# Four products at two levels instead of three, in three of the four down stages of a two-layer kernel

## The chip, the cores and the metric

The kernel runs on one core of one Trainium2 chip. Its time is the device time of one execution in microseconds, as the median of several runs. A profile is one more execution, recorded by the hardware profiler. The engines are TensorE (PE, matmuls; PEld are its weight loads), VectorE (DVE), ScalarE (ACT), GpSimd (POOL) and SyncE (SP), which issues every DMA of this kernel in one queue, in program order.

## The reference, cut to what matters

A layer of linear attention (A) and a gated layer (B) stand in turn, twice, each behind a layer norm and with a residual. The change touches layer B only. Here x is 2048 x 1024, w_gate and w_up are 1024 x 3584, w_down is 3584 x 1024, all in bf16.

```python
def _B_ref(x, w_gate, w_up, w_down):
    g = jnp.einsum("bsd,df->bsf", x, w_gate)
    u = jnp.einsum("bsd,df->bsf", x, w_up)
    h = g * u
    return jnp.einsum("bsf,fd->bsd", h, w_down)

x = A_x
x = x + _A_ref(_layernorm(x, axis=-1), A_wqkv, A_wo)
x = x + _B_ref(_layernorm(x, axis=-1), B_w_gate, B_w_up, B_w_down)
x = x + _A_ref(_layernorm(x, axis=-1), A_wqkv, A_wo)
x = x + _B_ref(_layernorm(x, axis=-1), B_w_gate, B_w_up, B_w_down)
```

## The kernel before

**How it is put together.** Every instruction is added by `_Prog.add` (line 50) to the queue of its engine, in the order of the program text; `plan` (line 105) then works out from the ranges that each one reads and writes which semaphores it has to wait for. Nothing is reordered. So the order of the `P.add` calls is the order on each engine, and a DMA whose wait is long holds up all DMAs that were added after it.

**The stages.** Layer B works on the tokens in two halves of 1024. For each half a gate/up stage (`gateup`, line 1786) makes h in the tile blocks hA, hB, hC, hD (two halves of tokens by two halves of the 3584 columns), and a down stage (`down`, line 1864) multiplies h by w_down and adds the result to x. The text calls the four down stages D0 (first layer B, first half), D1 (first layer, second half), D2 and D3 (second layer). Behind D0 and D2 comes the gate/up stage of the second half, behind D1 the second layer A; D3 ends the kernel.

**Seven products.** Each 2 x 2 block product is done with seven block products in place of eight (Strassen-Winograd). They are numbered 1 to 7; a down stage takes them in the order of the string in `DPROD` (line 730). At one level a product is 4 tiles of 128 tokens by 14 matmuls of 512 columns (line 2154), accumulated in one PSUM bank a tile; the banks run on from product to product in a chain, and after some products a bank's sum leaves PSUM: `stt` (line 841) on DVE scales it, adds a tile of x (or an earlier sum) and writes an f32 tile `rtmp` or x itself. For the products that `DTWO` (line 731) names, each of the blocks is split once more in seven (`two_level`, line 2016): 98 matmuls of 256 columns (line 2049). That needs sums of the blocks of h (`a_sums`, line 1902, four DVE operations a product, into the buffers of `s_buf`, line 1894) and sums of the blocks of the weights. Chosen so before: no product of D0, and products 5, 3 and 2 of D1, D2 and D3.

**The weights.** The four blocks of w_down and the four one-level sums of them (products 5, 6, 7 and 4) are in DRAM; the latter, the scratch tensor `t_scratch`, are made during the first gate/up stage (`wd_load`, `wd_prep`, `wd_store`, lines 939 to 952). `ring_issue` (line 785) loads the next weight unit into one of five slots of 8 KB a partition: half a one-level product (896 KB, written 4/0 and 4/1 below), or one of four parts a to d of a two-level one (3136 KB together). The sums for the second level lie in a further scratch tensor, `d_scratch`, one block a product, and are made once: those for 5 and 3 during D0 (`b_load`, `b_sums`, `b_store`, lines 1921 to 1952, called from `prep_step`, line 1977), those for 2 in D1 from weights loaded for that purpose (`b2_prep`, line 1954). An entry "-" in the list of units (`d_units`, line 736) takes a slot and loads nothing.

**What else runs in these stages.** Tiles of x are stored to a scratch tensor (`stash`, line 751) and loaded again in the `tail` of the next gate/up stage (line 1846), since the room is wanted for other things meanwhile. `sp_load` (line 775) fetches the sums of x for the next gate/up stage's second level. In D2 `x_pop` (line 871) runs the operations of `x_ops` (line 860), which make the sums of the normalized x for the next gate/up stage; `t1` to `t4` are the four of 2048 elements a partition. `dticks0` (line 2228) is called after each tile of D0 and D2 and `dticks1` (line 2257) after each tile of D1 and D3; they hold these loads, stores and pops. `tt` (line 838) is a DVE operation of two tensors, `dma` (line 439) the helper under which all DMAs appear.

## Time and the profile before

| | |
|---|---|
| time, median of 3 runs | 1435.49 us (1435.11 to 1437.32) |
| span of the profiled execution | 1433.4 us |
| that execution's clock of TensorE | 1.000 over the whole span |
| busy PE / DVE / ACT / POOL | 1422.9 / 1140.8 / 700.2 / 225.6 us |
| mean DMA rate, share of 16 engines | 230 GB/s, 76.8% |
| D0, D1, D2, D3 start at | 402.24, about 652, 1109.57, 1350.01 us |

The span is the profiled execution's own time from its first to its last instruction; the page gives no other time for it. It lies 2.1 us under the median of the runs. A busy time is a sum over the stages; whether an engine has room in one stage is read from that stage's window. In section 5 of the page a group is a line of the code, an engine and an operation, with busy time, mean of one in ns and the idle time before it with what ended it. L839 is the line of `tt`, L842 that of `stt`, L440 that of `dma`, so these groups hold operations from many places, and are told apart by their tiles and forms.

### The profile page before, as it was taken

The page shows a single profiled execution, that of the slowest core. Times are in us where ns is not written, and L with a number is a line of the kernel's source. Part 1 is how long each engine was busy: PE and PEld are TensorE (multiplying, and loading weights), DVE is VectorE, ACT ScalarE, POOL GpSimd, SP SyncE. Part 2 cuts the span into 40 slices and gives each one's busy share as a digit, 9 for nine tenths or more (in the row PEclk, how much of TensorE's full clock was granted, in tenths as well). Part 3 has the DMA queues.
Part 4 walks back from the last instruction along what each step waited for, and adds up shares of the span by engine and source line. Part 5 has one row for each costly group of instructions (what it writes and reads, how often), then busy time and mean ns, then how long its engine had stood idle before and what let it go on. Part 6 is the DMA issues. An engine that isn't in the chain of part 4 may idle for free.

```text
span 1433.4 us, 22057 instructions
## 1 busy us (share of the span) xinstructions
PE 1422.9 (99%) x8248; PEld 801.1 (56%) x8304; DVE 1140.8 (80%) x2048; ACT 700.2 (49%) x1478; POOL 225.6 (16%) x265
## 2 busy tenths in 40 slices
PE   9999999999999999999999999999999999999999
PEld 4444444555544555554664444456666477666548
DVE  7878887888867799877678878779877787777856
ACT  4752367766710255550156523667776016777401
POOL 4643632000000000000034345300000000000000
PEclk9999999999999999999999999999999999999999
DMA  7416867987889899986898067689976699777657
GB/s 235 108 26 188 180 136 192 285 290 256 291 282 343 258 270 290 273 274 234 247 358 225 28 175 166 131 236 275 283 244 205 223 300 314 260 261 257 205 163 241
DMA packets 386091, 330.00 MB, mean 230 GB/s; under 512 B 178368, under 2 KB 333888, under 8 KB 385472
## 3 DMA queue, kind: packets, MB, share of 16 engines
q1 hardware_dynamic: 385984, 328.59, 76.8%
q8 instruction: 65, 1.06, 0.3%
q14 instruction: 42, 0.34, 0.1%
HBM read 240.71 MB, written 64.23 MB: 213 GB/s over the span
## 4 chain that ended last, share of the span: by engine, by line
PE 96%; DVE 2%; ACT 1%; issue 1%; DMA 0%; POOL 0%; SPq 0%; ACTq 0%
PE ps L1584 27%; PE ps L1654 18%; PE ps L2154 16%; PE ps L1494 8%; PE ps L1396 8%; PE ps L1162 6%; PE ps L2049 6%; PE ps L966 5%; PE ps L976 3%; DVE arena L839 1%; PE ps L1408 1%; PE ps L1436 0%; DVE arena L842 0%; ACT arena L492 0%; DMA arena<-in_B_w_gate_dram 0%
## 5 line engine op out<-in xcount | busy, mean ns | idle before, releaser
L839 DVE TENSOR_TENSOR arena<-arena 128x512 f16<-128x512 f16 (+9 forms) x776 | 429.2, 579 | 74.3 <-ACT arena L1698 45.1
L1584 PE MATMUL ps<-arena 128*128 128x512 f16 x1808 | 446.8, 379 | 0.6 <-ACT ps L1614 0.6
L842 DVE SCALAR_TENSOR_TENSOR arena<-ps,arena 128x512 f16<-128x512 f32 (+2 forms) x440 | 293.2, 684 | 75.4 <-PE ps L2154 52.2
L1654 PE MATMUL ps<-arena 128*128 128x256 f16 x2324 | 312.1, 273 | 0.8 <-ACT arena L1698 0.6
L1654 PEld LDWEIGHTS ps<-arena 128*128 128x128 f16 (+1 forms) x2324 | 226.3, 98 | 104.1 <-DVE ps L1673 3.5
L1584 PEld LDWEIGHTS ps<-arena 128*128 128x128 f16 (+1 forms) x1808 | 176.5, 98 | 141.7 <-ACT ps L1614 1.1
L2154 PE MATMUL ps<-arena 128*128 128x512 f16 (+1 forms) x1053 | 229.9, 379 | 0.6
L1589 ACT ACTIVATE arena<-ps 128x512 f16<-128x512 f32 x224 | 134.0, 598 | 92.9 <-PE ps L1584 90.6
L2154 PEld LDWEIGHTS ps<-arena 128*128 128x128 f16 x1064 | 104.1, 98 | 124.7
L1670 ACT COPY ps<-ps 128x256 f32<-128x256 f32 x220 | 81.1, 369 | 127.5 <-PE ps L1654 121.3
L1673 DVE TENSOR_TENSOR ps<-ps,arena 128x256 f32<-128x256 f32 x220 | 92.1, 427 | 37.2 <-PE ps L1654 19.9
L1396 PE MATMUL ps<-arena 128*128 128x512 bf16 x499 | 114.1, 379 | 0.7
L2053 ACT COPY ps<-ps 128x256 f32<-128x256 f32 x36 | 12.9, 357 | 204.9 <-PE ps L2049 204.9
L1494 PE MATMUL ps<-arena 128*128 128x512 bf16 x500 | 110.7, 379 | 0.6
L483 POOL TENSOR_SCALAR arena<-arena 128x1 f32<-128x1 f32 x43 | 16.3, 380 | 589.9 <-DVE arena L482 589.9
L2049 PE MATMUL ps<-arena 128*128 128x256 f16 (+1 forms) x882 | 97.8, 273 | 0.1
L1162 PE MATMUL ps<-arena 128*128 128x512 bf16 (+1 forms) x412 | 94.7, 379 | 0.8 <-DVE ps L1166 0.3
L2049 PEld LDWEIGHTS ps<-arena 128*128 128x128 f16 x882 | 85.7, 98 | 11.9 <-DVE arena L842 0.7
L1302 POOL TENSOR_TENSOR arena<-arena 128x1024 f16<-128x1024 f32 x32 | 79.1, 2473 | 70.3 <-DVE arena L1300 61.6
L1614 ACT COPY ps<-ps 128x512 f32<-128x512 f32 x112 | 64.2, 573 | 50.0 <-PE ps L1654 45.2
L1001 POOL TENSOR_TENSOR arena<-arena 128x512 f32<-128x512 f32 x60 | 73.5, 1244 | 69.4 <-DVE arena L1091 33.7
L1494 PEld LDWEIGHTS ps<-arena 128*128 128x128 f16 x512 | 50.1, 98 | 59.8
(78 smaller groups left out, 1223.3 us busy)
## 6 DMA issues: line engine op xcount, KB each, us to landing
arena<-w_scratch SPq DMA_DIRECT2D x84, 512.0 KB, 5.1
arena<-sp_scratch SPq DMA_DIRECT2D x56, 512.0 KB, 5.9
arena<-t_scratch SPq DMA_DIRECT2D x29, 896.0 KB, 6.6
arena<-in_B_w_down_dram SPq DMA_DIRECT2D x20, 896.0 KB, 7.3
w_scratch<-arena SPq DMA_DIRECT2D x28, 512.0 KB, 6.2
sp_scratch<-arena SPq DMA_DIRECT2D x28, 512.0 KB, 4.1
arena<-in_B_w_gate_dram SPq DMA_DIRECT2D x42, 256.0 KB, 5.1
arena<-in_B_w_up_dram SPq DMA_DIRECT2D x42, 256.0 KB, 3.7
```

The costliest lines, as they stand in the source:

```text
L839: P.add("dve", lambda e: e.tensor_tensor(out=out, in0=a, in1=b, op=op), rd=rd, wr=wr, prd=prd)
L842: P.add("dve", lambda e: e.scalar_tensor_tensor(out=out, in0=a, scalar=sc, in1=b, op0=ALU.mult, op1=op1), rd=rd, wr=wr, prd=prd)
L1162: P.add("pe", lambda e: [e.matmul(psb(bank), x[:, k, :], w[:, k, :], start=(start and k == 0), stop=(k == 3), skip_group_check=True) for k ...
L1396: return [e.matmul(psb(bank), xr[:, t, j * 128:(j + 1) * 128], pk[:, h, t, :], start=(t == 0), stop=(t == NST - 1)) for t in range(NST)]
L1494: return [e.matmul(psb(bank), xnT[:, g, i * 128:(i + 1) * 128], wp[:, g, dh * 512:(dh + 1) * 512], start=(dh == 0 and g == 0), stop=(g == ...
L1584: P.add("pe", lambda e: [e.matmul(psb(bank), w[:, k, :], x[:, k, :], start=(start and k == 0), stop=(k == 3), skip_group_check=True) for k ...
L1589: P.add("act", lambda e: e.activation(t, psb(bank), AF.Copy, scale=SG), prd=[bank], wr=r)
L1654: P.add("pe", lambda e: [e.matmul(psb(bank)[:, 256 * half:256 * half + 256], w[:, k, :], xx[:, k, :], start=(start and k == 0), stop=(k == ...
L1670: P.add("act", lambda e: e.copy(psb(dst[c])[:, 0:256], lo), prd=[bk], pwr=[dst[c]])
L1673: P.add("dve", lambda e: e.tensor_tensor(out=psb(dst[c])[:, 256:512], in0=lo, in1=c5, op=ALU.add), prd=[bk], rd=rc5, pwr=[dst[c]])
L2049: P.add("pe", lambda e: [e.matmul(psb(bank)[:, 256 * half:256 * half + 256], a[:, k, :], w[:, k, :], start=(start and k == 0), stop=(k == ...
L2154: return [e.matmul(psb(bank), hv[:, 7 * hf + k, t * 128:(t + 1) * 128], w[:, k, :], start=(start and hf == 0 and k == 0), stop=(hf == 1 an ...
```

## The change

In D1, D2 and D3 the order of the products becomes 1, 6, 7, 2, 4, 5, 3, and product 4 is taken at two levels as 2, 5 and 3 were. D0 stays at one level with its order. What goes with it:

- The sums of weights for products 2 and 4 are both made in D0 (`r_sums`), from the ring slots in which these products' own weights lie, four DVE operations a product, spread over the first three tiles of the product, and one store in two DMAs after the third. `b2_prep` with its load in D1 is gone; `d_scratch` has a fourth block.
- The sums that leave PSUM behind products 1, 6 and 7 of D1 to D3, and 1, 7 and 4 of D0, are scaled and copied by ScalarE into `rtmp`, and GpSimd adds the tile of x (`evict_x`); for product 7 of D1 to D3 it makes two sums, one for product 4 and one for product 5.
- x tiles 1 to 7 instead of 3 to 7 are stashed and fetched again around the first layer's first half, 8 to 15 instead of 11 to 15 in D2, and 8 to 15 are fetched behind D3's gate/up stage. The buffers for the sums of h move.
- In D2 the loads of sums of x move from product 4 to product 5 (first two tiles), and the operations on x run in another order: t1 to t4 first, among products 2 and 4, then the rest.
- In the first gate/up stage the product tile `mb` and the copy tile get second buffers, one operation in each of two groups of the first pair comes later (`XD`), and `prep_s` takes two blocks in the other order.

The diff, cut to its core:

```diff
-    O_MB = O_X + 7 * D * 2
+    O_MB = {'2': O_X + 7 * D * 2, '3': O_X + 2 * D * 2}
...
-    dscr = nc.dram_tensor("d_scratch", (3, 128, NJ, 512), F16, kind="Internal").ap()
+    dscr = nc.dram_tensor("d_scratch", (4, 128, NJ, 512), F16, kind="Internal").ap()
...
-        L2D = "532"
-        DPROD = {(True, 0): "1274653", (True, 1): "1674253", (False, 0): "1674253", (False, 1): "1674253"}
-        DTWO = {(True, 0): "", (True, 1): "532", (False, 0): "532", (False, 1): L2D}
+        L2D = "5324"
+        DPROD = {(True, 0): "1274653", (True, 1): "1672453", (False, 0): "1672453", (False, 1): "1672453"}
+        DTWO = {(True, 0): "", (True, 1): L2D, (False, 0): L2D, (False, 1): L2D}
...
-                if first and ps_ and q in "742":
+                if first and ps_ and q == "7":
...
-                ts = zip([("t1", t1), ("t2", t2), ("t3", t3), ("t4", t4)], has("1"))
-                return [x for a in ts for x in a] + has("3") + has("2") + has("5")
+                return [("t1", t1), ("t2", t2), ("t3", t3), ("t4", t4)] + has("1") + has("3") + has("2") + has("5")
...
-                        (lambda tp=tp, rt=rt, a=b21, ra=r21: tt(tp[2], a, tp[1], ALU.subtract, ra + rt[1], rt[2]))]
+                ops = [(lambda tp=tp, rt=rt, a=b12, b=b11, ra=r12, rb=r11: tt(tp[0], a, b, ALU.subtract, ra + rb, rt[0])),
+                       (lambda tp=tp, rt=rt, a=b22, ra=r22: tt(tp[1], a, tp[0], ALU.subtract, ra + rt[0], rt[1])),
+                       (lambda a=b22, b=b12, ra=r22, rb=r12: tt(b, a, b, ALU.subtract, ra + rb, rb)),
+                       (lambda tp=tp, rt=rt, a=b21, ra=r21: tt(tp[2], a, tp[1], ALU.subtract, ra + rt[1], rt[2]))]
+                if jit:
+                    XD[q] = ops.pop(2)
+                res += ops
...
-            a11, a12, a21, a22 = w(0, 0), w(0, 1), w(1, 0), w(1, 1)
+            a11, a12, a21, a22 = w(0, 0), w(1, 0), w(0, 1), w(1, 1)
...
+                def o_cp(i):
+                    return O_X + D * 2 if first and ps_ == 0 and p % 2 and not i else O_CP + 2048 * i
...
+                        if jit and p == 0 and tk in ("P1B", "P5B"):
+                            XD[tk[1]]()
...
-                    for t in range(5):
-                        i = 8 * ps_ + 3 + t
+                    for t in range(1 if jit else 3 if first or not ps_ else 0, 8):
+                        i = 8 * ps_ + t
...
-                four = "4" in l2d
-                SB = {"5": O_HB if four else O_HC, "3": O_HC if four else O_HB if chain else O_HA, "2": RB, "4": RB}
+                SB = {"5": O_HB, "3": RB if first else O_HC, "4": RB if ps_ else O_X + 8 * D * 2}
+                s2 = 1024 if first else 0
 
                 def s_buf(q, i):
-                    if q == "2" and not first:
-                        return xnT[:, 0:7, 256 * i:256 * i + 256], lambda lo, hi: _seg(O_XT + 512 * i, 7, S * 2, 2 * lo, 2 * hi)
+                    if q == "2":
+                        c0 = s2 + 256 * i
+                        return xnT[:, 0:7, c0:c0 + 256], lambda lo, hi: _seg(O_XT + 2 * c0, 7, S * 2, 2 * lo, 2 * hi)
...
-                def b2_prep():
...
+                def r_sums(q):
...
+                    def nat(k, c):
+                        n = n_of[q, str(k)]
+                        o = r_slot(n)[0][0]
+                        return f(o, 3584).rearrange("p (j c) -> p j c", c=512)[:, :, 256 * c:256 * c + 256], _seg(o, 7, 1024, 512 * c, 512 * c + 512)
+
+                    def new(k, c):
+                        return vo_[:, k, :, 256 * c:256 * c + 256], ro(k, c)
+
+                    def op(o, a, b):
+                        tt(o[0], a[0], b[0], ALU.subtract, a[1] + b[1], o[1])
+
+                    def store():
+                        di = L2D.index(q)
                         for h in range(2):
-                            dma(vn[:, h], wd_v[:, 7 * h:7 * h + 7, 1, 0:512], rg(h, 0, 512), KDB[h])
-
-                    def store():
-                        for h in range(2):
-                            dma(dscr[2][:, 7 * h:7 * h + 7, :], vo_[:, h], R(V_L2 + 256 + 32 * h, 32), KDS[h], rd=rg(h, 0, 512))
-
-                    def op(o, a, b):
-                        x, y = [(vn if nat else vo_)[:, k, :, 256 * c:256 * c + 256] for k, c, nat in (a, b)]
-                        r = sum([rg(k, 256 * c, 256 * c + 256) for k, c, _ in (a, b)], [])
-                        tt(vo_[:, o[0], :, 256 * o[1]:256 * o[1] + 256], x, y, ALU.subtract, r, rg(o[0], 256 * o[1], 256 * o[1] + 256))
-                    return load, [lambda: op((0, 0), (0, 1, 1), (0, 0, 1)), lambda: op((0, 1), (1, 1, 1), (0, 1, 1)),
-                                  lambda: op((1, 1), (1, 1, 1), (0, 0, 0)), lambda: op((1, 0), (1, 0, 1), (1, 1, 0))], store
+                            dma(dscr[di][:, 7 * h:7 * h + 7, :], vo_[:, h], R(V_L2 + 128 * di + 32 * h, 32), KDW[2 * "24".index(q) + h], rd=ro(h, 0) + ro(h, 1))
+                    return [lambda: op(new(0, 0), nat(0, 1), nat(0, 0)), lambda: op(new(0, 1), nat(1, 1), nat(0, 1)),
+                            lambda: op(new(1, 1), nat(1, 1), new(0, 0)), lambda: [op(new(1, 0), nat(1, 0), new(1, 1)), store()]]
...
+                    if q in "24":
+                        for f in r_sums(q)[[0, 1, 3, 4][t]:[1, 3, 4, 4][t]]:
+                            f()
...
-                def chain_step(q, t, bank, pb):
+                def evict_x(t, bank, k, *xs):
+                    P.add("act", lambda e: e.activation(rtmp[k], psb(bank), AF.Copy, scale=CD), prd=[bank], wr=rr(k))
+                    for k2, (x, rx) in xs:
+                        P.add("pool", (lambda k2, x: lambda e: e.tensor_tensor(out=rtmp[k2], in0=rtmp[k], in1=x, op=ALU.add))(k2, x), rd=rx + rr(k), wr=rr(k2))
+
+                def chain_step(q, t, bank):
                     r = [rh(x, t) for x in (O_HA, O_HB, O_HC, O_HD, RB)]
                     a, b, c, d, e_ = [v[:, :, t * 128:(t + 1) * 128] for v in (hA, hB, hC, hD, hE)]
                     if q == "1":
                         tt(e_, a, d, ALU.subtract, r[0] + r[3], r[4])
-                        xs, rx = xq(0, 0, t)
-                        stt(rtmp[t], pb, CD, xs, rx, rr(t), prd=[bank])
...
+                        evict_x(t, bank, t, (t, xq(0, 0, t)))
                         tt(a, c, e_, ALU.subtract, r[2] + r[4], r[0])
-                        if first and ps_ and t == 0:
-                            b2_load()
...
                     elif q == "6":
-                        xs, rx = xq(0, 1, t)
-                        stt(rtmp[4 + t], pb, CD, xs, rx, rr(4 + t), prd=[bank])
+                        evict_x(t, bank, 4 + t, (4 + t, xq(0, 1, t)))
                         tt(a, b, a, ALU.subtract, r[0] + r[1], r[0])
-                        if first and ps_:
-                            b2_sums[t]()
-                            if t == 3:
-                                b2_store()
-                    elif q == "7":
-                        xs, rx = xq(1, 1, t)
-                        stt(rtmp[8 + t], pb, CD, xs, rx, rr(8 + t), prd=[bank])
-                        if four:
-                            xs, rx = xq(1, 0, t)
-                            stt(rtmp[12 + t], pb, CD, xs, rx, rr(12 + t), prd=[bank])
-                        if not first:
-                            ex_pop(1)
                         tt(d, d, c, ALU.add, r[3] + r[2], r[3])
                     else:
-                        xs, rx = xq(1, 0, t)
-                        stt(xs, pb, CD, xs, rx, rx, prd=[bank])
-                        final(1, 0, t)
+                        evict_x(t, bank, 8 + t, (12 + t, xq(1, 0, t)), (8 + t, xq(1, 1, t)))
                         ex_pop(1)
...
-                    if q == "6" and l2d and not chain:
-                        EX.extend(a_sums("5"))
-                    if q == ("4" if first else "7") and chain:
+                    if q == "7" and chain:
                         EX.extend(a_sums("2"))
...
-                        if q == "6" and l2d and t < 2:
-                            ex_pop(2)
                         if q == "1":
-                            xs, rx = xq(0, 0, t)
-                            stt(rtmp[t], pb, CD, xs, rx, rr(t), prd=[bank])
+                            evict_x(t, bank, t, (t, xq(0, 0, t)))
                             tt(ha, ha, hd, ALU.subtract, ra + rd_, ra)
                         elif q == "2":
                             xs, rx = xq(0, 0, t)
...
                             final(0, 0, t)
                             tt(hd, hd, hc, ALU.add, rd_ + rc, rd_)
                         elif q == "7":
-                            xs, rx = xq(1, 1, t)
-                            stt(rtmp[t], pb, CD, xs, rx, rr(t), prd=[bank])
+                            evict_x(t, bank, t, (t, xq(1, 1, t)))
                             tt(ha, hc, ha, ALU.subtract, ra + rc, ra)
                         elif q == "4":
-                            xs, rx = xq(1, 0, t)
-                            stt(rtmp[4 + t], pb, CD, xs, rx, rr(4 + t), prd=[bank])
+                            evict_x(t, bank, 4 + t, (4 + t, xq(1, 0, t)))
...
-                    for k in range(5):
-                        stash(11 + k)
-                if q == "4" and t < 2 and not first:
+                    for k in range(11 if first else 8, 16):
+                        stash(k)
+                if q == "5" and t < 2 and not first:
                     sp_load(1, t, "12")
                     if t == 0:
                         sp_load(1, 0, "53")
                 if first and q in "65":
                     x_pop(3 if q == "5" else 2)
-                elif not first and q in "453":
-                    x_pop({"4": [2, 2, 2, 2], "5": [0, 0, 0, 1], "3": [1, 2, 3, 3]}[q][t])
+                elif not first and q in "2453":
+                    x_pop({"2": [0, 1, 0, 1], "4": [0, 1, 0, 1], "5": [0, 0, 0, 1], "3": [2, 2, 3, 3]}[q][t])
...
-                for k in range(5):
-                    stash(3 + k)
+                for k in range(1 if first else 3, 8):
+                    stash(k)
```

## What is expected of the change, before it was run

> **What bounds the kernel now.** I read the page first, then the chain of work that ended last, then the order of time on TensorE (PE) and on the DMA queue of SyncE (SP).
>
> ```profile
> span 1433.4 us, 22057 instructions
> ...
> PE 96%; DVE 2%; ACT 1%; issue 1%; DMA 0%; POOL 0%; SPq 0%; ACTq 0%
> ```
>
> The reader is to see that PE is the bound: 96% of the chain is matmuls. An edit on another engine gains nothing by itself; only fewer columns through PE, or a wait of PE that comes or goes, moves the time. I call the four down stages D0 and D1 (first layer B, two halves of the tokens), D2 and D3 (second layer B). PE does not wait in them, but for the end of D2:
>
> ```profile
> 402.24 77.00 PE L2154 MATMUL ps<-arena 128*128 128x512 bf16 x353
> ...
> 1109.57 48.29 PE L2154 MATMUL ps<-arena 128*128 128x512 bf16 x222
> 1157.70 30.40 PE L2049 MATMUL ps<-arena 128*128 128x256 bf16 x273
> ```
> ```profile
> 1398.30 32.23 PE ps L2049 x294
> ```
>
> The first three rows are PE in order of time, the last one a piece of the chain. A one-level product is 56 matmuls; four of them start at 1109.57 and the next group at 1157.70, so one takes 48.13 / 4 = 12.03 us. A two-level product is 98 matmuls of half the width; three take 32.23 us in D3, so one takes 10.74. **One product moved to two levels saves 1.29 us**, in D1, D2 and D3 alike: 3 x 1.29 = 3.9 us, if every load and sum is there in time. That is the whole gain on the path. (The D2 row counts 273 because next-stage matmuls cut in later.)
>
> **What the engines beside PE get.** In D0 twelve, and in D1 to D3 twelve each, evictions of a product leave VectorE (DVE): 48 in all become 48 copies on ScalarE (ACT) and 60 adds on GpSimd (POOL: 12 in D0, 16 in each other stage, since product 7 feeds two).
>
> ```profile
> L842 DVE SCALAR_TENSOR_TENSOR arena<-ps,arena 128x512 f16<-128x512 f32 (+2 forms) x440 | 293.2, 684 | 75.4 <-PE ps L2154 52.2 <-PE ps L1584 16.3 <-PE ps L2049 3.1
> L1589 ACT ACTIVATE arena<-ps 128x512 f16<-128x512 f32 x224 | 134.0, 598 | 92.9 <-PE ps L1584 90.6 <-DVE arena L839 0.2
> L1001 POOL TENSOR_TENSOR arena<-arena 128x512 f32<-128x512 f32 x60 | 73.5, 1244 | 69.4 <-DVE arena L1091 33.7 <-DVE arena L1080 31.7 <-DVE arena L671 3.7
> ```
>
> DVE loses 48 x 0.684 = 33 us, ACT gains 48 x 0.598 = 29, POOL 60 x 1.244 = 75. None of it is on the path: the windows of these stages below show ACT at 0 and 2.2 us and POOL at 0. A bank is needed again one product (12 us) later; ACT frees it 0.6 us after its last matmul, and POOL needs at most 2 x 1.244 of every 3 us. I put this edit at 0. The second buffers in D0's gate/up stage (mb, cp), the two late operations of its first pair and the swapped blocks of prep_s count 0 too: same operations, and PE has no wait there. So do the five more tiles that are stashed and fetched again, except for two that stand in D0's way.
>
> **D0, where the new sums are made.** All products stay at one level, so PE gains nothing. Sums for products 2 and 4 are now taken from the ring slots while these products run, eight DVE operations, and four stores of 896 KB go out; product 2 used to be prepared in D1. Two more x tiles come back at the start.
>
> ```profile
> 419.05 0.29 DVE L839 TENSOR_TENSOR arena<-arena 128x256 f16<-128x256 f16 x1 [1.32 <-DMA arena<-t_scratch]
> ...
> 447.90 0.29 DVE L839 TENSOR_TENSOR arena<-arena 128x256 f16<-128x256 bf16 x1 [2.41 <-DMA arena<-in_B_w_down_dram]
> ```
> ```profile
> 424.88 1.83 SPq L440 DMA_DIRECT2D arena<-t_scratch  x2
> 426.75 2.81 SPq L440 DMA_DIRECT2D x_scratch<-arena  x5
> 429.61 3.31 SPq L440 DMA_DIRECT2D d_scratch<-arena  x4
> 439.93 3.28 SPq L440 DMA_DIRECT2D arena<-in_B_w_down_dram  x4
> 443.25 1.06 SPq L440 DMA_DIRECT2D arena<-t_scratch  x2
> ```
> ```profile
> arena<-t_scratch SPq DMA_DIRECT2D x1, 896.0 KB, 4.6
> ...
> arena<-t_scratch SPq DMA_DIRECT2D x1, 896.0 KB, 7.2
> ```
> ```profile
> 426.40:438.50 12.10, 12.10 (x58) 5.49 (x57) 9.14 (x13) 0.00 (x0) 0.00 (x0) 1.00 0.94 351
> ```
>
> The first fence is DVE, the second SP, in order of time; the third has the us to landing of the DMAs issued at 424.88 (into an empty queue) and at 443.25. SP issues in program order: weight halves 4/1 and 6/0 (424.88), stashes, the sums of 5 (429.61), the loads for the sums of 3, which reuse that buffer and so wait for the stores until 439.93, and only then 6/1 (443.25). That half lands at 443.25 + 7.2 = 450.45. Products start 12.07 apart (402.24, so product 6, the fifth, at 450.5), and 6/1 is wanted after seven matmuls, 1.5 us in, at 452.0. **The margin today is 1.6 us.** The window (columns: PE, PEld, DVE, ACT, POOL, clock, DMA share, GB/s) shows the DMA engines 94% busy in product 7: 351 / 0.94 = 373 GB/s when full.
>
> After the change the store of the sums of 2 is emitted ahead of 4/1 and waits for DVE. DVE stands in its queue until the loads for the sums of 5 have come (419.05; 1.4 later with 0.52 MB more in front). From there to the fourth sum of 2 it does three updates of hA and hD, three pairs for the sums of 5, the four new sums and two evictions. In a row each costs its duration less some 0.08 of overlap:
>
> ```profile
> L839 DVE TENSOR_TENSOR arena<-arena 128x1792 f16<-128x1792 f16 x16 | 17.3, 1080 | 0.0
> L839 DVE TENSOR_TENSOR arena<-arena 128x1536 f16<-128x1536 f16 x4 | 3.8, 950 | 3.8 <-DMA arena<-t_scratch 3.8
> ```
>
> That is 3 x 1.0 + 3 x 1.1 + 4 x 1.0 + 2 x 0.61 = 11.5, and 0.2 for the small piece at 419.05: the store leaves at 432.2, where 4/1 left at 424.88. So the queue is 7.3 us late, and 1.84 MB more are in it, 4.9 us at 373 GB/s. 6/1 comes 12.2 us later against a margin of 1.6: **PE waits 10.6 us.** Next, the loads for 3 are late by the same 12.2, so DVE, which they released at 447.90, is free at 460.1; four sums of 4, two pairs of 3 and two updates (4.0 + 2.2 + 2.0) end at 468.3, the two stores of 4 take 4.9, and behind them half 5/1 takes 2.5, and 2.1 are fixed (4.6 alone, less 2.5): 477.8, wanted at 462.6 + 1.5 = 464.1. That is 13.7 late in all, the first wait included. I know of no further wait behind it: the last two products bring no sums. Bounds: with queues that run at 420 GB/s and DVE released 1.4 sooner 8; with one more us for each DVE wait 15. I take 12.
>
> **D2, where the DMA engines are full.**
>
> ```profile
> 1157.70:1168.50 10.80, 10.66 (x98) 9.30 (x97) 9.20 (x14) 2.17 (x6) 0.00 (x0) 1.00 1.00 302
> ```
> ```profile
> 1150.01 0.87 SPq L440 DMA_DIRECT2D arena<-sp_scratch  x2
> ```
> ```profile
> 1162.19 0.35 DVE ps L2056
> ...
> 1162.59 12.41 PE ps L2049 x112
> ...
> 1183.33 4.83 DMA arena<-in_B_w_gate_dram
> ...
> 1188.21 0.61 PE ps L1654 x4
> ```
>
> The last fence is the chain: the first matmul of the next gate/up stage, amid product 3, already starts only when its weights land (1183.33 + 4.83 = 1188.16). A two-level product moves 3.21 MB (3136 KB of weights and sums) and 0.52 MB of output, in 10.74 us: 347 GB/s, where the full queue gave 302. A fourth one takes 12.4 us of queue in 10.74, 1.6 too long. And the sp loads of 0.52 MB, two of them in the second fence and a third one behind, move from the light product 4 into product 5: 1.57 / 0.302 = 5.2 us more. Together the gate weights come 6.8 us later than PE wants them. DVE is late too: the four x sums of 2048 now stand between two-level products, 1.2 us each, in front of the join on which PE waits (1162.19 above, a stop of 0.3 us); two such stops of about 0.9 would lie inside the DMA wait. Against 6.8 stand 1.29 saved and up to 1 us of slack: +4.5, bounds +1 (sp loads at 400 GB/s, some slack) and +6.
>
> **D1 and D3** have no sp loads, D1 no output and D3 no stage behind it. In D3 the queue needs 12.4 us a product as well, but product 3's loads are followed by nothing: 1 us at worst. I take -1.3 each, bounds -1.3 and +0.5. The x tiles that D3 reloads (8 for 5) are wanted only by POOL.
>
> **Sum.** 12 - 1.3 + 4.5 - 1.3 = +13.9 on a span of 1433.4. The median, 1435.5, lies 2.1 above that span: **1449.4 us**. My bounds add to +6.4 (1441.9) and +22 (1457.5), all ends at once.
>
> [...] The first ten matmuls of the program took 4.4 us, where ten take 10 x 12.03 / 56 = 2.15 in D2:
>
> ```profile
> L447 PE MATMUL ps<-arena 128*128 128x512 f16 x10 | 4.4, 631 | 1.4 <-POOL arena L443 1.4
> ```
>
> [...] By the row a restart costs 2.2 us; after the long waits of D0 and D2 that is +4.4, a rival below.
>
> ```profile
> 741.00:822.00 81.00, 80.58 (x369) 36.60 (x376) 66.74 (x110) 51.41 (x91) 37.91 (x41) 1.00 0.54 155
> ```
> ```profile
> L839 DVE TENSOR_TENSOR arena<-arena 128x1024 f16<-128x1024 f16 x12 | 8.9, 745 | 0.0
> ```
> ```profile
> L839 DVE TENSOR_TENSOR arena<-arena 128x1024 f16<-128x1024 f16 x11 | 7.5, 681 | 0.0
> ```
>
> The first row is a stretch with POOL busy for 37.91 of 81 us, the second one a group in it, the third the same form at 970 to 1100 us, where the page shows POOL at 0: 64 ns apart. [...] If each of the twelve adds of D0 blocked DVE for 1.24 us, some four of them ahead of the sums of 4, D0 would be 5 us worse; by the row it is 0.1.
>
> **Rivals, with chances.**
> Forecast, D0 and D2 stall: 1449.4, chance 0.60, own range 1442 to 1456.
> Half clock after the long waits: +4.4, 1453.8, 0.08. For it the start row; against it, no long wait elsewhere.
> GpSimd blocks DVE: +5, 1454.4, 0.06.
> Faster: every load is there in time, in D0 because DVE, freed of 8.2 us of evictions, sums earlier than I count, in D2 because the lead of four slots covers the sp loads: -3.9, 1431.6, 0.15. It decides at 6/1: if the lateness on SP stays below 1.6 us there is no wait. Against it: DVE is held by a load, not by evictions.
> Only D2 stalls, mildly (D0 covered): 0 - 1.3 + 3 - 1.3, 1435.9, 0.11. That also covers the case that the change does not do what it says, for instance a fourth product whose saving is eaten by its joins.
> So faster by over 0.2% (2.9 us, about what a measurement can tell) 0.15, within it 0.11, slower 0.74. The range runs from 1438 to 1456: the forecast, both dearer rivals and a D0 at a third of its price lie in it.
>
> **What will show it.** In D0: a PE wait of several us in front of the second half of product 6, released by a DMA from t_scratch, and a second one in product 5; the first store of sums on SP near 432. In D2: product 3 starting late on w_down or d_scratch, and the gate weights landing well behind 1188 plus the shift. In D1 and D3: 10.7 us for each of four products without a gap. I am wrong if 6/1 is issued before 445, or if the sp loads land without pushing product 3's weights.

## The result and the profile after

| | before | after |
|---|---|---|
| time, median | 1435.62 us (1435.11 to 1437.32, 4 runs) | 1459.61 us (1458.07 to 1461.08, 4 runs) |
| span of the profiled execution | 1433.4 us | 1457.5 us |
| mean clock of TensorE | 1.000 | 0.995 |

The ratio of the times is 1.0164, with a 95% interval of 1.0152 to 1.0177: the changed kernel is **24.0 us slower** by the medians. The forecast was 1449.4 us (1438 to 1456): the right sign, some 10 us short.

The page of the changed kernel, first the span, then the chain of work by engine, then the new group of adds on POOL (count, busy us, mean ns):

```profile
span 1457.5 us, 22516 instructions
...
PE 88%; DVE 5%; DMA 3%; issue 1%; SPq 1%; ACT 1%; POOL 0%; DVEq 0%
...
L2106 POOL TENSOR_TENSOR arena<-arena 128x512 f32<-128x512 f32 x60 | 95.6, 1602 | 595.8 <-ACT arena L2104 377.7
```

PE was 96% of the chain and is 88%: waits have come in. Where they are is told by the first matmul of each down stage. PE in order of time (start, length, line), before:

```profile
645.10 1.46 PE L2154 MATMUL ps<-arena 128*128 128x512 bf16 x6
...
1350.01 1.24 PE L2154 MATMUL ps<-arena 128*128 128x512 bf16 x5
```

(402.24 and 1109.57 stand in the prediction; D1's first matmul is thus at 645.10, not at about 652.) After:

```profile
404.99 1.24 PE L2148 MATMUL ps<-arena 128*128 128x512 bf16 x5
...
666.75 0.59 PE L2148 MATMUL ps<-arena 128*128 128x512 bf16 x2
...
1129.54 1.67 PE L2148 MATMUL ps<-arena 128*128 128x512 bf16 x7
...
1375.65 1.67 PE L2148 MATMUL ps<-arena 128*128 128x512 bf16 x7
```

The differences of these starts, and of the last one to the end of the span, give the length of each stretch. A stretch from one down stage to the next holds the stage behind it too.

| stretch | before | after | change | forecast |
|---|---|---|---|---|
| start to D0 | 402.24 | 404.99 | +2.75 | 0 |
| D0 to D1 | 242.86 | 261.76 | +18.90 | +12 |
| D1 to D2 | 464.47 | 462.79 | -1.68 | -1.3 |
| D2 to D3 | 240.44 | 246.11 | +5.67 | +4.5 |
| D3 to the end | 83.4 | 81.9 | -1.5 | -1.3 |
| sum | 1433.4 | 1457.5 | +24.1 | +13.9 |

The gain is there in D1 and D3, and the loss lies in three places. PE in order of time after the change shows them; the bracket is the idle time before a group and what ended it.

```profile
246.10 0.61 PE L1661 MATMUL ps<-arena 128*128 128x256 f16 x4 [1.08 <-DVE arena L841]
...
250.90 0.61 PE L1661 MATMUL ps<-arena 128*128 128x256 f16 x4 [0.52 <-DVE arena L841]
...
279.87 0.83 PE L1661 MATMUL ps<-arena 128*128 128x256 f16 x6 [0.48 <-DVE ps L1680]
...
443.75 12.26 PE L2148 MATMUL ps<-arena 128*128 128x512 f16 x56 [0.65 <-DMA arena<-t_scratch]
462.46 25.58 PE L2148 MATMUL ps<-arena 128*128 128x512 f16 x105 [6.45 <-DMA arena<-t_scratch]
494.10 6.79 PE L2148 MATMUL ps<-arena 128*128 128x512 bf16 x20 [6.06 <-DVE arena L841]
...
1181.90 10.87 PE L2061 MATMUL ps<-arena 128*128 128x256 f16 x98 [0.64 <-DVE ps L2068]
1193.64 12.57 PE L2061 MATMUL ps<-arena 128*128 128x256 f16 x112 [0.87 <-DVE ps L2068]
1208.11 2.47 PE L2061 MATMUL ps<-arena 128*128 128x256 bf16 x21 [1.90 <-DMA arena<-in_B_w_down_dram]
1212.49 0.61 PE L1661 MATMUL ps<-arena 128*128 128x256 f16 x4 [1.92 <-DMA arena<-in_B_w_gate_dram]
...
1218.64 2.03 PE L1661 MATMUL ps<-arena 128*128 128x256 f16 x16 [1.62 <-DVE arena L841]
```

There are three waits in the first gate/up stage. In D0 one of 6.45 us stands ahead of the second half of product 6 (weights) and one of 6.06 ahead of product 3 (DVE). Five stand in D2 and behind it; they add to 6.95 us, and less the 1.29 saved that is 5.66, all that the stretch got longer. And a second thing: 105 matmuls behind the first long wait take 25.58 us, where 105 x 12.03 / 56 = 22.6 were to be expected. The windows behind the two long waits (columns: length, then PE, PEld, DVE, ACT, POOL busy, granted clock, DMA share, GB/s) say why:

```profile
462.46:467.98 5.52, 5.52 (x14) 1.94 (x14) 5.52 (x8) 0.00 (x0) 0.00 (x0) 0.50 0.56 192
...
494.10:498.78 4.68, 4.68 (x11) 1.67 (x11) 2.80 (x6) 0.00 (x0) 0.00 (x0) 0.50 0.62 231
```

The clock is 0.50 over these 5.52 and 4.68 us: 14 + 11 matmuls at 0.215 would take 5.4 us and took 10.2, so 4.8 us are lost in D0 beside its 13.2 us of waits.

### The profile page after: what moved, and what is told of

It reads as the page before. It is cut to its first block, busy times and chain, and to the rows that moved or that the text cites. A ratio compares the mean times of both kernels' runs of the same rounds, so it can differ in the third digit from the quotient of the medians.

```text
span 1457.5 us, 22516 instructions
## 1 busy us (share of the span) xinstructions
PE 1425.3 (98%) x8374; PEld 814.5 (56%) x8430; DVE 1165.5 (80%) x2028; ACT 735.5 (50%) x1544; POOL 322.5 (22%) x325
## 3 DMA queue, kind: packets, MB, share of 16 engines
q8 instruction: 66, 1.08, 0.3%
## 4 chain that ended last, share of the span: by engine, by line
PE 88%; DVE 5%; DMA 3%; issue 1%; SPq 1%; ACT 1%; POOL 0%; DVEq 0%
PE ps L1591 25%; PE ps L1661 17%; PE ps L2148 12%; PE ps L1400 8%; PE ps L2061 7%; PE ps L1498 6%; PE ps L1166 6%; PE ps L970 5%; DVE arena L841 3%; PE ps L980 3%; DMA arena<-t_scratch 1%; DVE arena L844 1%; DMA d_scratch<-arena 1%; SPq L441 1%; DMA arena<-in_B_w_down_dram 0%
## 5 line engine op out<-in xcount | busy, mean ns | idle before, releaser
L841 DVE TENSOR_TENSOR arena<-arena 128x512 f16<-128x512 f16 (+9 forms) x792 | 478.7, 634 | 108.3 <-ACT arena L1705 45.4
L844 DVE SCALAR_TENSOR_TENSOR arena<-ps,arena 128x512 f16<-128x512 f32 (+2 forms) x392 | 259.8, 686 | 31.1 <-PE ps L1591 16.3
L2106 POOL TENSOR_TENSOR arena<-arena 128x512 f32<-128x512 f32 x60 | 95.6, 1602 | 595.8 <-ACT arena L2104 377.7
L2148 PE MATMUL ps<-arena 128*128 128x512 f16 (+1 forms) x885 | 199.2, 386 | 13.9 <-DMA arena<-t_scratch 7.1
L2148 PEld LDWEIGHTS ps<-arena 128*128 128x128 f16 x896 | 88.7, 99 | 122.8 <-DMA arena<-t_scratch 8.1
L2061 PE MATMUL ps<-arena 128*128 128x256 f16 (+1 forms) x1176 | 130.2, 273 | 3.5 <-DMA arena<-in_B_w_down_dram 1.9
L1677 ACT COPY ps<-ps 128x256 f32<-128x256 f32 x220 | 81.1, 369 | 103.7 <-PE ps L1661 96.1
L2061 PEld LDWEIGHTS ps<-arena 128*128 128x128 f16 x1176 | 114.3, 98 | 19.0 <-DVE ps L2068 2.3
L2104 ACT ACTIVATE arena<-ps 128x512 f32<-128x512 f32 x48 | 28.7, 597 | 133.8 <-PE ps L2148 133.8
L1005 POOL TENSOR_TENSOR arena<-arena 128x512 f32<-128x512 f32 x60 | 73.5, 1244 | 69.4 <-DVE arena L1095 33.7
L1498 PEld LDWEIGHTS ps<-arena 128*128 128x128 f16 x512 | 50.1, 98 | 59.8
```

The lines of the kernel that those rows point to most:

```text
L841: P.add("dve", lambda e: e.tensor_tensor(out=out, in0=a, in1=b, op=op), rd=rd, wr=wr, prd=prd)
L844: P.add("dve", lambda e: e.scalar_tensor_tensor(out=out, in0=a, scalar=sc, in1=b, op0=ALU.mult, op1=op1), rd=rd, wr=wr, prd=prd)
L1498: return [e.matmul(psb(bank), xnT[:, g, i * 128:(i + 1) * 128], wp[:, g, dh * 512:(dh + 1) * 512], start=(dh == 0 and g == 0), stop=(g == ...
L2061: P.add("pe", lambda e: [e.matmul(psb(bank)[:, 256 * half:256 * half + 256], a[:, k, :], w[:, k, :], start=(start and k == 0), stop=(k == ...
L2106: P.add("pool", (lambda k2, x: lambda e: e.tensor_tensor(out=rtmp[k2], in0=rtmp[k], in1=x, op=ALU.add))(k2, x), rd=rx + rr(k), wr=rr(k2))
L2148: return [e.matmul(psb(bank), hv[:, 7 * hf + k, t * 128:(t + 1) * 128], w[:, k, :], start=(start and hf == 0 and k == 0), stop=(hf == 1 an ...
```

## The experiments

The table of all runs first, with the stretches of each run's profile, PE's waits of 0.25 us and more in D0, and the time lost at clock 0.50 in D0. The time of e8_best is the median of 8 executions and that of e9_tail of 11; the others are one execution each. On the same chips the kernel before took 1437.56 us (e1 to e4, one execution), 1435.64 (e5 to e8, 11) and 1436.0 (e9 and e10, 15), so two rows can differ by some 2 us for that alone.

| run | time, us | D0 to D1 | D2 to D3 | PE waits in D0, us | lost at half clock, us |
|---|---|---|---|---|---|
| after | 1459.61 | 261.76 | 246.11 | 0.65, 6.45, 6.06 | 4.8 |
| e1_fill | 1458.20 | 259.93 | 245.59 | 0.43, 0.33, 0.25, 1.11 (two filled) | none |
| e2_actq | 1457.13 | 257.62 | 246.10 | 6.17, 4.63 | yes |
| e3_ranges | 1454.90 | 260.51 | 244.54 | 6.43, 7.32 | yes |
| e4_pops | 1466.12 | 260.43 | 252.86 | 6.56, 0.94, 6.30 | yes |
| e5_early | 1445.27 | 247.95 | 246.13 | 3.45 | yes |
| e6_d2three | 1454.82 | 261.55 | 240.16 | 0.29, 6.21, 6.23 | yes |
| e7_evict | 1437.07 | 242.86 | 240.17 | none | none |
| e8_best | 1439.66 | 249.34 | 240.17 | 4.14 | yes |
| e9_tail | 1434.82 | 243.00 | 240.17 | none | none |
| e10_undo_evict | 1465.04 | 263.66 | 246.45 | 0.48, 6.81, 2.05, 4.45 | yes |

The start of D0 moves by up to 2.5 us between runs whose code ahead of it is the same (404.81 in e5 to 407.35 in e10), so the stretches tell more than a single time. PE's stop of 0.58 us at the head of the gate/up stage moves with it (243.19 and 244.67), and the wait at 279.87 lasts between 0.22 and 1.51 us.

**Is the slow clock a consequence of the waits?** Extra matmuls fill them:

```diff
+                            if first and not ps_ and t == 0 and (q, hf) in FILL:
+                                fb, fnum = FILL[q, hf]
+                                P.add("pe", lambda e, fb=fb, fnum=fnum, fw=wsl[0][0]: [e.matmul(psb(fb), hA[:, 0, 0:128], fw[:, 0, :], start=True,
...
+                FILL = {("6", 1): (B_DV[0], 28), ("3", 0): (B_DX[0], 38)}
```

> The changed kernel with idle PE time filled in D0: 28 extra matmuls (results unused) ahead of the second half of product 6 and 38 ahead of product 3, where PE waited 6.45 and 6.06 us and then ran one matmul per 0.43 us in place of 0.216. Theory 'a long idle halves the clock': the extra matmuls keep PE busy, all matmuls behind them step by 0.216 us, and the slow stretches (3.0 us behind the first wait, 2.5 behind the second) are gone. The second wait ends when VectorE has worked off what a store held up, so only the second stretch shortens the path: 1459.6 - 2.5 = about 1457, clock 1.000. Rival 'the slow steps come from something else (weights, power)': steps of 0.43 us stay and the time stays at 1459.6 or more.

PE in order of time, with the extra matmuls (L2154) at 456.27 and 486.91:

```profile
456.27 6.21 PE L2154 MATMUL ps<-arena 128*128 128x512 f16 x28
462.73 12.26 PE L2149 MATMUL ps<-arena 128*128 128x512 f16 x56 [0.25 <-DMA arena<-t_scratch]
476.11 10.75 PE L2149 MATMUL ps<-arena 128*128 128x512 f16 x49 [1.11 <-DMA arena<-t_scratch]
486.91 8.15 PE L2154 MATMUL ps<-arena 128*128 128x512 bf16 x37
494.89 4.70 PE L2149 MATMUL ps<-arena 128*128 128x512 bf16 x20
```

56 matmuls take 12.26 us right behind the fill, and the last 20 take 4.70 in place of 6.79. The slow clock is gone (the mean clock is 1.000 in place of 0.995), with the same weights and the same transfers: here the idling brought it. The stretch gets 1.8 us shorter and no more, because the waits stay where data are late; and the wait for half 5/1 that the prediction had put at 3.1 us appears here with 1.11, once PE is no longer slowed ahead of it.

**Who holds half 4/1 back?** The four new stores are issued by ScalarE, so that they no longer stand ahead of it on SyncE:

```diff
-                            dma(dscr[di][:, 7 * h:7 * h + 7, :], vo_[:, h], R(V_L2 + 128 * di + 32 * h, 32), KDW[2 * "24".index(q) + h], rd=ro(h, 0) + ro(h, 1))
+                            P.add("act", (lambda h: lambda e: e.dma_start(dscr[di][:, 7 * h:7 * h + 7, :], vo_[:, h]))(h),
+                                  rd=ro(h, 0) + ro(h, 1), wr=R(V_L2 + 128 * di + 32 * h, 32), dma_sem=KDW[2 * "24".index(q) + h])
```

> The changed kernel with the four stores of the new sums (products 2 and 4) issued by ScalarE in place of SyncE, same bytes, same order of sums. Theory 'SyncE's order is the price': half 4/1 is no longer held behind a store that waits for VectorE, it is issued some 8 us sooner, and only the added bytes delay 6/1 (1.84 MB at 373 GB/s = 4.9 us less the margin of 1.6): PE waits at most 3.3 us ahead of the second half of product 6, the wait ahead of product 3 falls below 2, no slow matmuls; D0 to D1 lasts 261.8 - 13 = about 249 us, total about 1447. Rival 'the bytes are the price, the queue is full': waits of 6 us stay, total within 2 us of 1459.6.

The first wait stayed (6.17 us), as the rival said, but not for its reason. SyncE's queue in order of time, first of the changed kernel, then of this run:

```profile
430.07 5.05 SPq L441 DMA_DIRECT2D d_scratch<-arena  x2
435.16 1.71 SPq L441 DMA_DIRECT2D arena<-t_scratch  x2
...
454.21 0.91 SPq L441 DMA_DIRECT2D arena<-t_scratch  x2
```

```profile
431.83 4.99 SPq L441 DMA_DIRECT2D arena<-t_scratch  x2
```

With no store ahead of them, 4/1 and 6/0 still leave at 431.83 and 436.50, against 424.88 and 426.39 in the kernel before; in the changed kernel they left at 435.16 and 435.76, so only 4/1 gained. There are five ring slots, and 4/1 is the fifth unit behind 2/0, 6/0 the fifth behind 2/1: they load into the slots that `r_sums` reads. PE is done with product 2 long before, but VectorE, which was itself waiting for the loads of the sums of 5, is not. The stretch got 4.1 us shorter all the same: the wait ahead of product 3 fell to 4.63 us, and less was lost at half clock.

**Sums one product sooner.** If the slots are the price, VectorE must read them sooner: the sums of 2 during product 1, where it idles, those of 4 during product 7.

```diff
-                    if q in "24":
-                        for f in r_sums(q)[[0, 1, 3, 4][t]:[1, 3, 4, 4][t]]:
+                    if q in "17":
+                        for f in r_sums({"1": "2", "7": "4"}[q])[[0, 0, 1, 3][t]:[0, 1, 3, 4][t]]:
```

> The changed kernel, where VectorE makes the sums of 2 during product 1 and those of 4 during product 7, one product sooner; both stores go out one product sooner too; same operations, same bytes. In the run with ScalarE's stores, halves 4/1 and 6/0 still waited for VectorE (issued 431.83 and 436.50): they load into the ring slots that the sums are read from. Theory 'VectorE holds the slots': with the slots free in time 4/1 leaves SyncE some 7 us sooner, the wait ahead of the second half of product 6 (6.45 us) falls to at most 2, the one ahead of product 3 (6.06) to at most 2, no slow matmuls: D0 to D1 lasts 243 to 247 us in place of 261.8, total about 1443. Rival 'the added bytes hold the queue': both waits stay above 4 us, total 1456 or more.

The queue and PE:

```profile
427.45 1.84 SPq L441 DMA_DIRECT2D arena<-t_scratch  x2
```

```profile
480.73 6.17 PE L2148 MATMUL ps<-arena 128*128 128x512 bf16 x20 [3.45 <-DVE arena L844]
```

Same operations and bytes; 4/1 leaves 7.7 us sooner, the wait ahead of product 6 is gone, the stretch is 13.8 us shorter and the time 1445.3. With e2, where the stores alone did not bring it, that shows the cause of the first wait: VectorE's sums of 2 came too late. One wait of 3.45 us is left, ahead of product 3, and even behind that one 20 matmuls take 6.17 us where 4.70 is normal.

**The first gate/up stage.** The operation that `XD` puts off writes one quarter of a block of x, and PE's seven small products all waited for the whole block. They get the range of their own quarter:

```diff
-                    b11, b12, b21, b22 = [(x[:, 2 * k:2 * k + 2, 256 * c:256 * c + 256], rx) for k in range(2) for c in range(2)]
+                    xo, xst = (O_T, 1024) if q == "5" else (O_XT + (0 if q == "1" else 4 * S * 2) + (s0 + (512 if q == "3" else 0)) * 2, S * 2)
+                    b11, b12, b21, b22 = [(x[:, 2 * k:2 * k + 2, 256 * c:256 * c + 256], _seg(xo + 2 * k * xst, 2, xst, c * 512, (c + 1) * 512))
+                                          for k in range(2) for c in range(2)]
```

> The changed kernel, where each of the seven small products of a two-level product in gate/up now waits for its own block of x and not for the whole x block. Theory 'the postponed operation of the first pair holds up PE, which doesn't need its block yet': the PE waits of 1.08 and 0.52 us at 246.1 and 250.9 shrink to at most 0.2 each, gate/up before D0 is 1.4 to 1.6 us shorter, total about 1458. Rival 'VectorE is late with blocks that PE does need': the waits stay, total 1459.6.

```profile
245.09 0.60 PE L1663 MATMUL ps<-arena 128*128 128x256 f16 x4
...
1214.50 1.81 PE L1663 MATMUL ps<-arena 128*128 128x256 f16 x14 [0.53 <-DVE arena L841]
```

The groups that waited 1.08 and 0.52 us start with no wait (the first one is the first row), and D0 starts 1.5 us sooner. The same edit takes the last wait behind D2 from 1.62 to 0.53 us. That stretch went from 246.11 to 244.54, but 0.56 of it is the wait for w_down, 1.34 instead of 1.90, which the edit does not touch (in e1 it was 1.37). So some 1.6 us in the gate/up stage and 1.1 in D2 were waits for parts of a block that PE did not need yet.

**D2: joins, VectorE, or the queue?** The four 2048-element sums of x move from the two-level products 2 and 4 to product 6:

```diff
-                    x_pop({"2": [0, 1, 0, 1], "4": [0, 1, 0, 1], "5": [0, 0, 0, 1], "3": [2, 2, 3, 3]}[q][t])
+                    x_pop({"6": [1, 1, 1, 1], "5": [0, 0, 0, 1], "3": [2, 2, 2, 1]}[q][t])
```

> The changed kernel with the four 2048-element sums of x of D2 moved from products 2 and 4 (two-level, with joins on VectorE) to product 6 (one-level). Theory 'the joins behind these sums are on the path': the PE waits of 0.64 and 0.87 us in D2 are gone and the stage is 1.5 us shorter, total about 1458. Rival 'the DMA queue sets the end of D2': the waits go, but those for w_down and the gate weights (1.90 and 1.92 us) grow by the same amount, total 1459.6.

A miss: the stretch is 6.7 us longer. The joins' waits did go, but PE got a new one, and lost 2.65 us at half clock behind it (49 matmuls in 13.40 us, where e1 took 10.75):

```profile
1161.32 13.40 PE L2148 MATMUL ps<-arena 128*128 128x512 f16 x49 [5.55 <-DVE arena L841]
```

```profile
1144.77 18.62 DVE L841 TENSOR_TENSOR arena<-arena 128x1792 f16<-128x1792 f16 x14 [1.66 <-PE ps L2148]
```

DVE runs 14 sums back to back in 18.62 us, and PE starves. Ten are of 1792 elements and four are the moved ones of 2048; alone they take 1.08 and 1.21 us, but four of the fourteen took 2.04 to 2.17. In D2 the one-level products have no room on DVE either. Why some take so long, the groups of DVE's sums in D2's product 7 show, first of the changed kernel, then of a run with all evictions back on DVE (e10, below):

```profile
L841 DVE TENSOR_TENSOR arena<-arena 128x1792 f16<-128x1792 f16 x7 | 12.8, 1856 | 0.1
```

```profile
L841 DVE TENSOR_TENSOR arena<-arena 128x1792 f16<-128x1792 f16 x5 | 5.3, 1083 | 0.0
```

1856 against 1083 ns: with the adds on POOL beside them, the sums take some 0.8 us longer on the mean. The adds suffer too; POOL's groups, in product 7 of D2 and in a stretch of D0 where DVE waits:

```profile
L2106 POOL TENSOR_TENSOR arena<-arena 128x512 f32<-128x512 f32 x8 | 13.2, 1665 | 1.9 <-ACT arena L2104 1.6
```

```profile
L2106 POOL TENSOR_TENSOR arena<-arena 128x512 f32<-128x512 f32 x4 | 4.6, 1153 | 8.1 <-ACT arena L2104 8.1
```

**Were the evictions worth moving?** Two runs: the move alone on the kernel before (e7), and its undoing in the changed one (e10), whose edit this is; e7's is the reverse:

```diff
                 def evict_x(t, bank, k, *xs):
-                    P.add("act", lambda e: e.activation(rtmp[k], psb(bank), AF.Copy, scale=CD), prd=[bank], wr=rr(k))
                     for k2, (x, rx) in xs:
-                        P.add("pool", (lambda k2, x: lambda e: e.tensor_tensor(out=rtmp[k2], in0=rtmp[k], in1=x, op=ALU.add))(k2, x), rd=rx + rr(k), wr=rr(k2))
+                        stt(rtmp[k2], psb(bank), CD, x, rx, rr(k2), prd=[bank])
```

> The kernel before, with only the evictions of 1, 6 and 7 (D1 to D3) and of 1, 7 and 4 (D0) moved to ScalarE with the add on GpSimd. Theory 'this edit is off the path': each of the four stage lengths within 0.3 us of before, total within 0.2% of before. Rival 'adds on GpSimd and sums on VectorE shut each other out': VectorE's sums of 1792 that overlap an add take about 2.0 us in place of 1.08, VectorE is late for the first two-level product and PE waits there, some 1 to 3 us in D1 to D3 each, total 1438 to 1444.

> The changed kernel with all evictions back on VectorE (one operation from PSUM with the x tile, two for product 7), as the kernel before had them; nothing on ScalarE and GpSimd. Theory 'the move to GpSimd buys nothing, since each add shuts VectorE out for about as long as the eviction took': D1, D2 and D3 keep their lengths to 0.5 us, VectorE's sums of 1792 take 1.08 us throughout. Rival 'VectorE has no room for them beside the fourth product': VectorE comes late to the joins and D1 to D3 get 1 us or more longer each, total 1462 or more.

The move alone changes D0 to D1 and D2 to D3 by 0.0 and -0.3 us, D1 to D2 by +0.6 (465.07 against 464.47), with one PE stop of 0.52 on a load of layer A's weights. Without it the changed kernel's D1, D2 and D3 stretches are 0.5, 0.3 and 0.7 us longer, D0's 1.9. By these two profiles, one each, it is worth about a microsecond and a half in D1 to D3 of the changed kernel and costs at most 0.6 us on the path of the kernel before; neither theory's large effect was there.

**D2 as it was before**, three two-level products with its loads, stashes and x operations; D0, D1 and D3 stay changed:

```diff
-        DPROD = {(True, 0): "1274653", (True, 1): "1672453", (False, 0): "1672453", (False, 1): "1672453"}
-        DTWO = {(True, 0): "", (True, 1): L2D, (False, 0): L2D, (False, 1): L2D}
+        DPROD = {(True, 0): "1274653", (True, 1): "1672453", (False, 0): "1674253", (False, 1): "1672453"}
+        DTWO = {(True, 0): "", (True, 1): L2D, (False, 0): "532", (False, 1): L2D}
```

> The changed kernel with D2 as it was before: three two-level products, product 4 at one level, loads of sums of x at product 4, x operations and stashes as before; D0, D1 and D3 stay changed. Theory 'the fourth product doesn't fit into D2's 32 us of VectorE and of the DMA queue': D2 to D3 lasts 240.4 us as before in place of 246.1, total 1453.9. Rival 'the evictions on ScalarE and GpSimd cost there': D2 keeps 2 us or more of its loss.

240.16 us in place of 246.11, with the evictions still on ScalarE and GpSimd: the fourth product and what it moves cost D2 all of its 5.7 us.

**Together.** Sums sooner, own ranges, and D2 as before:

> The changed kernel with three edits together: sums of 2 and 4 made one product sooner, blocks of x waited for one by one in gate/up, and D2 as before. If the three theories hold, D0 costs at most 4 us more than before, the first gate/up stage and D2 nothing, D1 and D3 gain 1.5 us each: 1432.5 to 1437. If a wait of D0 only moves elsewhere, 1440 or more.

1439.66 us (8 runs), 1.0026 [1.0015, 1.0037] of before: a wait only moved elsewhere. It stands ahead of product 3; PE and DVE of this run:

```profile
479.64 5.57 PE L2158 MATMUL ps<-arena 128*128 128x512 bf16 x14 [4.14 <-DVE arena L841]
```

```profile
466.84 1.56 DVE L841 TENSOR_TENSOR arena<-arena 128x2048 f16<-128x2048 f16 x2 [6.42 <-DMA d_scratch<-arena]
```

DVE stands 6.42 us in front of the first operation on x for the next stage (`t1`). It writes the buffer that the store of the sums of 3 still reads, and the evictions on which product 3 waits are queued behind it. So the next run takes these operations out of product 6, and lets the store of 4 go last:

```diff
-                if first and q in "65":
-                    x_pop(3 if q == "5" else 2)
+                if first and q == "5":
+                    x_pop(5)
...
+                        r_sums("4")[4]()
```

> The kernel of the run before this one (sums of 2 and 4 one product sooner, blocks of x one by one, D2 as before) with two more edits in D0: the operations on x for the next gate/up stage all stand at product 5 (five a tile) and none at product 6, and the store of the sums of 4 goes out behind that of the sums of 3. Theory 'the first operation on x writes the buffer that the store of the sums of 3 still reads, and blocks VectorE': the PE wait of 4.14 us ahead of product 3 and the 2.3 us of slow matmuls behind it are gone, D0 to D1 lasts 242.9 to 243.6 us, total about 1433.3, 0.1 to 0.2% under before. Rival 'a wait comes back in front of the gate/up matmuls, since the x operations are later': D0 to D1 stays above 246, total 1436 or more.

```profile
404.80 77.35 PE L2159 MATMUL ps<-arena 128*128 128x512 bf16 x357
```

PE runs through D0 with no wait, as before the change (77.00 us). The time is 1434.82 us (11 runs) against 1436.0 of the kernel before (15 runs): **0.9984 [0.9975, 0.9993]**, 0.16% faster than before, some 2 us, and 25 us faster than the change as made. In the profile the gain is in D1 to D2 (462.78 against 464.47) and from D3 to the end (82.4 against 83.4). Which of the two edits in D0 did it was not tried apart.

## Why the prediction was right and wrong

**D1 and D3, -1.3 each: right.** -1.68 and -1.5. PE's saving is what the counting of matmuls said, where loads and sums are in time.

**The evictions, 0: right as a price** (e7), **wrong in its reason.** The prediction took from the two groups, 64 ns apart, that the adds on POOL cost DVE 0.1 us in D0. In D2's product 7 both are slower beside each other: 1083 ns (e10) become 1856 on DVE, and 1153 (the stretch of D0) become 1665 on POOL. The rows that were compared were means, and they hid the effect: of the twelve sums of the first, only one started while an add ran on POOL, and it took 1.46 us where the others took 0.67 to 0.69.

```profile
789.02 1.46 DVE L839 TENSOR_TENSOR arena<-arena 128x1024 f16<-128x1024 f16 x1
```

In D0 the slowed sums lay in time in which DVE then waited for loads anyway (11.51 us ahead of 456.08); in e4 the slower and the moved sums together starved PE for 5.55 us.

**The first gate/up stage, 0: wrong**, by the step "same operations, and PE has no wait there". The operations are the same, but two of them now come behind a matmul, and PE's next products waited for the whole block. From PE's 0.58 us stop at the stage's head to D0 it measured +2.6 us (243.13 to 404.99, against 242.96 to 402.24); e3 takes 1.7 of it (243.35 to 403.48). The rest, about 0.9 us, was not taken apart; the wait at 279.87, which the kernel before does not have, is part of it.

**D0, +12: the first wait came, with a second holder.** The prediction said the store holds SyncE in front of 4/1; e2 shows that the ring slots hold 4/1 and 6/0 as well. The store's second half and the slot of 6/0 wait for the same VectorE sum, the fourth of 2, so the time came out nearly right, in part by luck: 6/1 was forecast to land at 462.65 (450.45 + 12.2) and landed at 462.41. But the cure that follows from it, e2, left the wait at 6.17. The wait was 6.45 instead of 10.6, since PE itself came later by the 2.75 us of the stage ahead, by 0.65 at 4/1 and by smaller stops. **The step that failed is "I know of no further wait behind it".** The 3.1 us forecast at 5/1 did not come; in their place stood 6.06 ahead of product 3, by way of `t1` and the buffer of the store of 3 (e9 takes it out). In sum, waits of 13.2 against the 13.7 worked out: that the size agreed is luck, since half of it stood elsewhere. The 12 that was taken is 1.7 below the prediction's own working.

**The half clock, a rival at 0.08 and +4.4: it happened.** It cost 4.8 us, at clock 0.50, both times in D0; D2's waits of 1.90 and 1.92 us left the clock at 1.00, so that the sizes agree is luck in part. The +4.4 was an estimate, twice what the first ten matmuls of the program took above ten in D2 (4.4 against 2.15 us); that a wait brings such a cost no run of the kernel before shows. The changed kernel showed it: 14 + 11 matmuls in 10.2 us in place of 5.4 behind its waits of 6.45 and 6.06. Against the rival the prediction argued only that no long wait stood elsewhere in the trace. That is no evidence: its own sum had just put a 10.6 us wait there. Every run with a wait of 3.45 us or more in D0 lost time at a slow clock (mean clock 0.993 to 0.998), so behind 10.6 us the rival belonged in the forecast.

**D2, +4.5: right in size, half right in its parts.** +5.67. The lateness of DMA was put at 6.8 and was 1.90 + 1.92 = 3.8. The two stops at the joins were seen (0.9 each, measured 0.64 and 0.87), but do not lie inside the DMA wait: they come before it, and the five waits add up to the loss. The wait of 1.62 for a block of x was not seen (e3). How much of the 3.8 is the moved loads of sums of x, and how much the fourth product, was not tried apart.

Of the 10.2 us missed, 6.9 are D0 (4.8 of them the clock, 1.7 the lower figure taken), 2.75 the stage ahead of it and 1.2 D2, less 0.6 in D1 and D3. So the time went wrong by a rival that was priced and kept out of the sum (4.8), by an edit priced at nothing without asking who waits for the moved operation (2.75), and by a term taken below its own working (1.7).

## What to carry to other kernels

A new reader of a ring slot is a new holder of it: count when the last engine is done with a buffer, not when the main one is, and make side products early, in the idle time of the engine that makes them. When a forecast has a long wait of PE, price the half clock behind it: every run here with a wait of 3.45 us or more in D0 had it, and one wait cost from 1.5 us (e5: 20 matmuls in 6.17 in place of 4.70) to 2.65 (e4: 49 in 13.40 in place of 10.75). And look at what each engine's queue carries behind a wait: here one operation for the next stage, stuck on a store, held the evictions of this one.

## What the runs showed of the hardware

Waits of PE were followed by a slow clock, but the length of one wait does not sort them. In the changed kernel the clock is 0.50 from 461.22 to 468.05 us and from 491.94 to 498.77, that is from within the waits of 6.45 and 6.06 us to some way behind them, and 1.00 ahead of and behind both stretches. Behind 3.45 us (e5, D0) the mean clock is 0.62 over 4.50 us, and behind 5.55 (e4, D2) 0.51 over 5.47. The profiled executions with a wait of 3.45 us or more in D0 have a mean clock of 0.993 to 0.998 over the whole span, the others one of 0.999 or 1.000. Of the shorter waits, 2.05 us (e10, D0) and 1.93 (e5, D2) were followed by slow matmuls too: 49 took 12.44 us, where e1 took 10.75, and 21 took 3.96, where the changed kernel took 2.47. 1.90 (the changed kernel, D2) and 2.88 (e10, D2) were not. PE of e10 and e5:

```profile
481.37 12.44 PE L2147 MATMUL ps<-arena 128*128 128x512 f16 x49 [2.05 <-DMA arena<-t_scratch]
...
1217.80 0.61 PE L1661 MATMUL ps<-arena 128*128 128x256 f16 x4 [2.88 <-DMA arena<-in_B_w_gate_dram]
```

```profile
1194.17 3.96 PE L2061 MATMUL ps<-arena 128*128 128x256 bf16 x21 [1.93 <-DMA arena<-in_B_w_down_dram]
```

Windows of e10 around its waits of 2.05 and 2.88 us, in the same columns as above:

```profile
479.25:482.67 3.42, 1.37 (x7) 0.60 (x7) 0.00 (x0) 0.00 (x0) 0.00 (x0) 1.00 1.03 329
482.67:486.08 3.41, 3.41 (x9) 1.20 (x8) 0.22 (x1) 0.00 (x0) 0.00 (x0) 0.50 1.01 414
...
1213.12:1216.53 3.41, 1.80 (x17) 1.36 (x14) 0.73 (x2) 0.00 (x0) 0.00 (x0) 1.00 1.05 304
1216.53:1219.95 3.42, 2.15 (x19) 1.72 (x20) 0.73 (x2) 0.65 (x2) 0.00 (x0) 1.00 1.05 331
```

The stretch that holds the wait of 2.05 us, with PE busy for 1.37 of 3.42 us, has clock 1.00 and the next one 0.50. The two over which the wait of 2.88 us lies, with PE busy for 1.80 and 2.15, have 1.00 both, and so have the 4.20 us from 1217.80 on. What decides whether the clock falls, and for how long, was not shown.
